# Decayed linear attention and a Mish layer: the first group's start in another order

## The chip, the cores and the metric

The kernel runs on one core of one Trainium2 chip. The metric is the device time of one execution in microseconds (us); lower is better. The kernel before takes 210.04 us, the median of 3 runs (209.95 to 210.83).

## The reference

Four sequences of 768 tokens and 8 heads of 64 go through linear attention with one decay per head, in blocks, and then through a layer with the activation h * tanh(softplus(h)), which is Mish. Cut to what matters:

```python
Dmask = np.where(rel >= 0, lam[:, None, None] ** rel[None], 0.0)
for b in range(nb):                              # blocks of a sequence
    intra = (einsum('bhic,bhjc->bhij', qb, kb) * Dmask) @ vb
    inter = einsum('bhid,bhde->bhie', qb * lam_pow, kv_state)
    out[:, :, block_b] = intra + inter
    kv_state = lam_block * kv_state + einsum('bhsd,bhse->bhde', kb * rev_pow, vb)
x = out, tokens by 512
h = x @ w_in                                     # 512 x 2048
return (h * tanh(softplus(h))) @ w_out           # 2048 x 512
```

## The kernel before, in words

The kernel takes blocks of 128 tokens, so a sequence has six, and the six make six **groups** of 4 x 128 tokens, one block from each of the four sequences. A block of one sequence is called a chunk here; chunks 0 to 3 are the first group. A chunk holds q, k and v of 8 heads, 128 tokens by 512 values. For each group the attention output is laid out transposed in `xt`; sixteen products with w_in (`mm1_unit`, into the bank `ph`, ended by Mish on ScalarE) and then products with w_out follow. The attention of the next group is laid between the products of this one. Only the first group has nothing to hide behind: its attention is the start of the kernel, and the change is about it.

The program order on every engine is written out by hand (a manual schedule), so each engine takes its instructions in the order of the code, and waits on semaphores for what others give.

The first group's decay is not taken from a running state, since the state is zero. Its mask is made whole instead: `decays` (line 182) makes rel * ln(lam) on VectorE, one piece for each of 8 heads, and ScalarE makes the exponential of four heads at a time (687, 690). The result is `dm`, in two halves t = 0 and 1. Then each chunk goes through three helpers:

- `first_t` (211) transposes k into the PSUM tile `pk` and q into `pq`, four products with the identity each; ScalarE copies pk to `pkT`, VectorE copies pq to `pqT`.
- `first_s` (228) makes the scores `pS`, eight products, and VectorE multiplies them with `dm` into `sb`, two instructions.
- `first_o` (241) makes `pO` from sb and v (`vz`), eight products, and ScalarE copies it to `xt`. pk, pq and pO have one bank each.

`busy(m)` (161) issues m products of zeros that nobody reads, 512 columns wide; they stand where TensorE would wait. Lines 684 to 713 set these in order. `mm1_part` (line 488 on) does a part of the products with w_in: for the first two tiles the 384 columns of chunks 0 to 2 are done ahead of the last `first_o`, or right behind it.

`pair_decays` (188) prepares the decay by pairs of heads, `lnp` on VectorE and its exponential `lbc` on ScalarE; `lk` (694) is the decay of k by position, from the iota `ek`. They are wanted only later, by `scale_k` and by the state's factor `lbm` (715 to 718).

All loads that turn 32-bit values into 16-bit ones go out from POOL (GpSimd) in the order of lines 125 to 146; one issue follows another on that engine. The chunks' k, q and v come first (line 69, 77, 80; 128 KB each), then w_in in four quarters `win` (the first of them in three pieces, of 128, 128 and 256 columns, line 93), then w_out in four quarters `wout`, then the second group. An issue takes its turn among eight semaphores, so that the ninth waits for the first to land. The first k and q come through SyncE and ScalarE (66, 74).

Of the kernel before, what the change touches and what calls it, by code (L numbers as in the profile page):

```python
# [20 lines left out]
def kernel(  # L21
# [62 lines left out]
    cuts = (0, 128, 256, DF // WS)  # L84
    win0 = [const.tile([128, NKC, b_ - a_], F16, name=f"win0{a_}") for a_, b_ in zip(cuts, cuts[1:])]
    win = [None] + [const.tile([128, NKC, DF // WS], F16, name=f"win{s}") for s in range(1, WS)]
    wout = [const.tile([128, NKI // WS, DMO], F16, name=f"wout{s}") for s in range(WS)]

    def load_win(s):
        w = DF // WS  # L90
        if s == 0:
            for t, a_, b_ in zip(win0, cuts, cuts[1:]):
                nc.gpsimd.dma_start(
                    out=t, in_=moe_w_in[:, a_:b_].rearrange("(k p) f -> p k f", p=128))
            return
        nc.gpsimd.dma_start(
            out=win[s],
            in_=moe_w_in[:, s * w : (s + 1) * w].rearrange("(k p) f -> p k f", p=128),
        )
# [31 lines left out]
    for f, i in ((load_q, 1), (load_v, 0), (load_k, 2), (load_q, 2)):  # L131
        f(i)
    nc.gpsimd.iota(ek, pattern=[[0, 1]], base=MID, channel_multiplier=-1,
                   allow_small_or_imprecise_dtypes=True)
# [26 lines left out]
    def busy(m):  # L161

        t = ps.tile([128, 4 * C], F32, name="busy", tag="ph", bufs=2)
        for _ in range(m):
            nc.tensor.matmul(t, kzero, kzero2, start=True, stop=True)  # L165
# [13 lines left out]
    lbc = const.tile([128, JP], F32, name="lbc")  # L179
    lqt = const.tile([128, H], F32, name="lqt")  # L180

    def decays(t):
        for j in range(JP):
# [4 lines left out]
    def pair_decays():  # L188
        lnh = lnb.rearrange("p (j t) -> p j t", t=2)
        for hp in range(2):  # L190
            rs = slice(64 * hp, 64 * hp + 64)
            nc.vector.tensor_copy(lnp[rs, :], lnh[rs, :, hp])
        nc.scalar.activation(lbc, lnp, AF.Exp, scale=float(C))
# [17 lines left out]
    def first_t(c):  # L211

        out_ = []
        for src, name in ((k0 if c == 0 else kn[c], "pk"), (q0 if c == 0 else qn[c], "pq")):
# [7 lines left out]
            if name == "pk":  # L222
                nc.scalar.activation(out_[-1], pt, AF.Copy)
# [264 lines left out]
    def mm1_part(n, ni, lo, hi):  # L488
# [4 lines left out]
        for kc in range(NKC):  # L493
            nc.tensor.matmul(  # L494
                ph_t[ni][:, lo:hi],
                win0[min(ni, 2)][:, kc, max(ni - 2, 0) * 128 : max(ni - 2, 0) * 128 + 128] if ni < w
                else win[ni // w][:, kc, (ni % w) * 128 : (ni % w) * 128 + 128],
# [185 lines left out]
    nh = len(first_halves)  # L683
    nc.scalar.activation(k0, kn[0], AF.Copy)
    decays(0)
    nc.vector.tensor_copy(q0, qn[0])
    nc.scalar.activation(dm[:, 0], dm[:, 0], AF.Exp)
    decays(1)
# [149 lines left out]
```

## Time and profile before

| what | value |
|---|---|
| median of 3 runs | 210.04 us (209.95 to 210.83) |
| the profiled execution | 210.5 us |
| its span, first to last instruction | 208.5 us |
| TensorE busy | 197.3 us (95%) |
| VectorE busy | 136.5 us (65%) |
| ScalarE busy | 90.2 us (43%) |
| POOL busy | 108.5 us (52%) |
| granted TensorE clock, mean | 0.984 |
| chain of waits, by engine | PE 73%, DVE 12%, DMA 6%, issue 4% |

In the profile, PE is TensorE's products, PEld its weight loads, DVE is VectorE, ACT is ScalarE, SP is SyncE. Times count from the span's start. A timeline row gives start, length, engine, line, operation, the tiles (out<-in), the shape and the count, and in brackets how long the engine had stood idle and what ended it. The profiled execution is one that was not among the three timed runs; terms worked out from its rows belong to its 210.5 us. "Granted clock" is the share of full speed that TensorE was given.

### The profile page before, as it was taken

The page shows a single profiled execution, that of the slowest core. Times are in us where ns is not written, and L with a number is a line of the kernel's source. Part 1 is how long each engine was busy: PE and PEld are TensorE (multiplying, and loading weights), DVE is VectorE, ACT ScalarE, POOL GpSimd, SP SyncE. Part 2 cuts the span into 40 slices and gives each one's busy share as a digit, 9 for nine tenths or more (in the row PEclk, how much of TensorE's full clock was granted, in tenths as well). Part 3 has the DMA queues.
Part 4 walks back from the last instruction along what each step waited for, and adds up shares of the span by engine and source line. Part 5 has one row for each costly group of instructions (what it writes and reads, how often), then busy time and mean ns, then how long its engine had stood idle before and what let it go on. Part 6 is the DMA issues. An engine that isn't in the chain of part 4 may idle for free.

```text
span 208.5 us, 4364 instructions
## 1 busy us (share of the span) xinstructions
PE 197.3 (95%) x1736; PEld 128.6 (62%) x1736; DVE 136.5 (65%) x253; ACT 90.2 (43%) x159; POOL 108.5 (52%) x132
## 2 busy tenths in 40 slices
PE   7598999999998999999999999999999999999993
PEld 2366544467644568845578845578755598544892
DVE  5747761577899998546997537995728784222543
ACT  4444768566672532044542055442065520366300
POOL 7997333799999799539997049970000000000000
PEclk9759999999999999999999999999999999999999
DMA  9999999999999399997999994999462222400023
GB/s 128 137 153 176 208 206 195 153 211 131 160 183 165 25 95 137 196 204 157 100 129 148 210 174 69 98 141 199 104 176 53 50 41 75 139 0 3 2 78 124
DMA packets 112470, 26.76 MB, mean 128 GB/s; under 512 B 102594, under 2 KB 111938, under 8 KB 112450
## 3 DMA queue, kind: packets, MB, share of 16 engines
q0 software_dynamic: 78080, 13.37, 87.7%
q1 hardware_dynamic: 31392, 10.49, 26.4%
q10 hardware_dynamic: 2978, 2.62, 4.1%
q8 instruction: 13, 0.21, 0.4%
q14 instruction: 7, 0.06, 0.1%
HBM read 27.26 MB, written 6.29 MB: 161 GB/s over the span
## 4 chain that ended last, share of the span: by engine, by line
PE 73%; DVE 12%; DMA 6%; issue 4%; POOL 2%; ACT 1%; ACTq 0%; DVEq 0%
PE ph L494 28%; PE z L599 13%; PE x L599 8%; PE y L599 7%; PE po L516 6%; DMA vz<-in_v_dram 4%; DVE sb L427 3%; DVE raw L393 2%; DVE xtok L446 2%; DMA qn<-in_q_dram 2%; PE fin L599 2%; DVE gsum L572 1%; PE pO L249 1%; PE pO L438 1%; PE pS L411 1%
## 5 line engine op out<-in xcount | busy, mean ns | idle before, releaser
L494 PE MATMUL ph<-xt,win 128*128 128x512 f16 (+2 forms) x404 | 88.6, 369 | 0.4 <-ACT hsg L508 0.2
L508 ACT ACTIVATE hsg<-ph 128x512 f16<-128x512 f32 x96 | 57.0, 597 | 70.4 <-PE ph L494 70.3
L494 PEld LDWEIGHTS <-win 128*128 128x128 f16 x404 | 37.0, 98 | 37.6 <-issue 0.6
L599 PEld LDWEIGHTS <-gsum 128*128 128x128 f16 x336 | 31.6, 98 | 3.5
L395 POOL TENSOR_TENSOR w<-raw,lbm 128x256 f16<-128x256 f32 x24 | 18.6, 805 | 16.7 <-DVE raw L393 16.7
L427 DVE TENSOR_TENSOR sb<-pS,maskT 128x512 f16<-128x512 f32 x32 | 19.8, 680 | 9.8 <-PE pS L411 9.8
L572 DVE TENSOR_TENSOR gsum<-hsg 128x1024 f16<-128x1024 f16 x20 | 18.6, 932 | 10.9 <-ACT hsg L508 10.9
L599 PEld LDWEIGHTS <-hsg 128*128 128x128 f16 x240 | 23.2, 98 | 3.7
L80 POOL DMA_DIRECT2D vz<-in_v_dram x24 | 21.9, 916 | 4.5 <-DMA win<-in_moe_w_in_dram 2.5
L69 POOL DMA_DIRECT2D kn<-in_k_dram x23 | 21.0, 914 | 4.9 <-DMA win<-in_moe_w_in_dram 2.4
L77 POOL DMA_DIRECT2D qn<-in_q_dram x23 | 20.9, 908 | 4.5 <-DMA wout<-in_moe_w_out_dram 3.3
L599 PE MATMUL x<-wout,hsg 128*128 128x256 f16 x160 | 19.6, 273 | 0.0
L599 PE MATMUL z<-tsum,gsum 128*128 128x256 f16 x160 | 19.1, 272 | 0.0
L264 DVE TENSOR_TENSOR ktil<-kn,lk 128x512 f16<-128x512 f16 (+1 forms) x12 | 11.3, 960 | 6.5 <-DMA kn<-in_k_dram 6.5
L516 PE MATMUL po<-wout,hsg 128*128 128x512 f16 x64 | 15.1, 379 | 0.0
L264 POOL TENSOR_TENSOR ktil<-kn,lk 128x512 f16<-128x512 f16 x12 | 13.2, 1103 | 0.0
L446 DVE TENSOR_TENSOR xtok<-pO,lqt 128x256 f16<-128x256 f32 x32 | 11.3, 412 | 0.9 <-PE pO L438 0.9
L393 DVE TENSOR_TENSOR raw<-pv,w 128x256 f32<-128x256 f32 x24 | 8.6, 414 | 4.6 <-PE pv L385 4.4
L516 PEld LDWEIGHTS <-hsg 128*128 128x128 f16 x64 | 6.0, 98 | 5.9
L599 PE MATMUL z<-tsum,hsg 128*128 128x256 f16 x80 | 9.6, 273 | 0.0
L650 DVE TENSOR_TENSOR u<-z,p 128x512 f32<-128x512 f32 x5 | 3.5, 692 | 9.0 <-PE z L599 9.0
L165 PE MATMUL busy<-kzero 128*128 128x512 f16 x18 | 7.9, 534 | 1.2 <-DVE kzero L150 1.2
(101 smaller groups left out, 220.1 us busy)
## 6 DMA issues: line engine op xcount, KB each, us to landing
out_dram<-osum SPq DMA_DIRECT2D x14, 256.0 KB, 2.5
vz<-in_v_dram POOLq DMA_DIRECT2D x24, 128.0 KB, 5.5
kn<-in_k_dram POOLq DMA_DIRECT2D x23, 128.0 KB, 5.4
qn<-in_q_dram POOLq DMA_DIRECT2D x23, 128.0 KB, 5.5
wout<-in_moe_w_out_dram POOLq DMA_DIRECT2D x4, 512.0 KB, 17.2
win<-in_moe_w_in_dram POOLq DMA_DIRECT2D x3, 512.0 KB, 10.9
out_dram<-osum ACTq DMA_DIRECT2D x5, 256.0 KB, 4.5
out_dram<-osb ACTq DMA_DIRECT2D x4, 256.0 KB, 5.9
```

Of the source, the lines that this page charges most:

```text
L69: nc.gpsimd.dma_start(out=kn[i], in_=chunk_rows(k, i))
L77: nc.gpsimd.dma_start(out=qn[i], in_=chunk_rows(q, i))
L80: nc.gpsimd.dma_start(out=vz[i % NVB][:, :, 0:D], in_=chunk_rows(v, i))
L264: (nc.vector if i <= B or 2 * B < i < 3 * B or i >= (NG - 1) * B else nc.gpsimd).tensor_tensor(out=t, in0=kn[i], in1=bc(lk, 2, D), op=ALU. ...
L395: nc.gpsimd.tensor_tensor(out=wst[b][hf][(n + 1) % 2], in0=raw, in1=lbm[:, hs, :], op=ALU.mult)
L427: nc.vector.tensor_tensor(out=s.sb[m][t], in0=sc[m][t], in1=bc(maskT, 1, JP), op=ALU.mult)
L446: nc.vector.tensor_tensor(out=xtok[m][:, :, t, :], in0=s.pO[t][:, m], in1=bc(lt[:, :, t], 2, D), op=ALU.mult)
L494: nc.tensor.matmul(ph_t[ni][:, lo:hi], win0[min(ni, 2)][:, kc, max(ni - 2, 0) * 128 : max(ni - 2, 0) * 128 + 128] if ni < w else win[ni // ...
L508: nc.scalar.activation(hsg[n][:, ni, :], ph_t.pop(ni), AF.Mish)
L516: nc.tensor.matmul(po, hsg[n][:, ki, b * C : (b + 1) * C], wout[part][:, kk, :], start=(ki == 0), stop=(ki == NKI - 1),)
L572: nc.vector.tensor_tensor(out=gsum[n, i][:, ks, :], in0=a, in1=b, op=op)
L599: nc.tensor.matmul(t, lhs(kk, b), rhs(kk, c, c + w), start=(fresh and kk == 0 and (alone or i == 0)), stop=(kk == HK - 1), skip_group_chec ...
```

## The change

Four things are changed, all in the start.

1. **Loads.** w_in's first quarter is one tile and one load, and it is issued ahead of the load of v of chunk 3; the iota ek comes right behind the iota rel.
2. **Decay.** The exponential of 128 * ln(lam) is made for all heads (`lbh`) right behind the logarithm, and so is `lk`; `pair_decays` only copies on VectorE, and stands behind the last products of the first group. Seven of the eight pieces of `decays` come before q's conversion, one behind it. The table for Mish is loaded right behind dm's second exponential.
3. **Order.** The transposes of chunk 1 come right behind the scores of chunk 0, and those of chunk 3 come before the pO of chunk 1.
4. **Zero products.** `busy` can be given a width. Of the products of 512 columns many are gone; products of 128 columns stand in the pauses: two before the first transposes, four between those of k and of q, four before the scores of chunk 2, two before the pO of chunk 2.

```diff
-    cuts = (0, 128, 256, DF // WS)
-    win0 = [const.tile([128, NKC, b_ - a_], F16, name=f"win0{a_}") for a_, b_ in zip(cuts, cuts[1:])]
-    win = [None] + [const.tile([128, NKC, DF // WS], F16, name=f"win{s}") for s in range(1, WS)]
+    win = [const.tile([128, NKC, DF // WS], F16, name=f"win{s}") for s in range(WS)]
...
-    for f, i in ((load_q, 1), (load_v, 0), (load_k, 2), (load_q, 2)):
-        f(i)
     nc.gpsimd.iota(ek, pattern=[[0, 1]], base=MID, channel_multiplier=-1,
                    allow_small_or_imprecise_dtypes=True)
-    for f, i in ((load_v, 1), (load_k, 3), (load_q, 3), (load_v, 2), (load_v, 3)):
+    for f, i in ((load_q, 1), (load_v, 0), (load_k, 2), (load_q, 2), (load_v, 1), (load_k, 3),
+                 (load_q, 3), (load_v, 2), (load_win, 0), (load_v, 3)):
         f(i)
-    for s in range(WS):
+    for s in range(1, WS):
         load_win(s)
...
-    def busy(m):
+    def busy(m, w=4 * C):
...
-            nc.tensor.matmul(t, kzero, kzero2, start=True, stop=True)
+            nc.tensor.matmul(t[:, 0:w], kzero, kzero2[:, 0:w], start=True, stop=True)
...
     def pair_decays():
-        lnh = lnb.rearrange("p (j t) -> p j t", t=2)
-        for hp in range(2):
-            rs = slice(64 * hp, 64 * hp + 64)
-            nc.vector.tensor_copy(lnp[rs, :], lnh[rs, :, hp])
-        nc.scalar.activation(lbc, lnp, AF.Exp, scale=float(C))
+        for src, dst in ((lnb, lnp), (lbh, lbc)):
+            lnh = src.rearrange("p (j t) -> p j t", t=2)
+            for hp in range(2):
+                rs = slice(64 * hp, 64 * hp + 64)
+                nc.vector.tensor_copy(dst[rs, :], lnh[rs, :, hp])
...
             if name == "pk":
+                if between:
+                    busy(between, C)
                 nc.scalar.activation(out_[-1], pt, AF.Copy)
...
+    nc.scalar.activation(lbh, lnb, AF.Exp, scale=float(C))
+    nc.scalar.activation(lk, lnb, AF.Exp, scale=ek)
     nc.scalar.activation(k0, kn[0], AF.Copy)
-    decays(0)
+    decays(0, range(JP))
+    decays(1, range(JP - 1))
     nc.vector.tensor_copy(q0, qn[0])
+    decays(1, range(JP - 1, JP))
     nc.scalar.activation(dm[:, 0], dm[:, 0], AF.Exp)
-    decays(1)
-    first_t(0)
+    busy(2, C)
+    first_t(0, between=4)
     nc.scalar.activation(dm[:, 1], dm[:, 1], AF.Exp)
+    nc.scalar.preload_act_table(AF.Mish)
     busy(1)
     first_s(0)
-    pair_decays()
-    nc.scalar.activation(lk, lnb, AF.Exp, scale=ek)
+    first_t(1)
     busy(2)
-    first_t(1)
-    nc.scalar.preload_act_table(AF.Mish)
-    busy(1)
     first_s(1)
     first_o(0)
-    busy(3)
     first_t(2)
-    busy(1)
+    busy(4, C)
     first_s(2)
+    first_t(3)
     first_o(1)
-    busy(3)
-    first_t(3)
+    busy(2, C)
     first_o(2)
-    busy(1)
     first_s(3)
     mm1_part(0, 0, 0, GT - C)
     first_o(3)
     mm1_part(0, 1, 0, GT - C)
     scale_k(0)
+    pair_decays()
```

Three places in the engines' rows show what stands where. First ScalarE, from the logarithm (lnb) to the transposed k of chunk 1, before:

```order
L173 ACTIVATE lnb<-lamb 128x8
L684 ACTIVATE k_94<-kn_98 128x512
L687 ACTIVATE dm<-dm 128x512
L223 ACTIVATE pkT<-pk 128x512
L690 ACTIVATE dm<-dm 128x512
L193 ACTIVATE lbc<-lnp 128x4
L694 ACTIVATE lk<-lnb,ek 128x8
L223 ACTIVATE pkT<-pk 128x512
L697 ACT_TABLE_LOAD
L251 ACTIVATE xt<-pO 128x4x128
```

The same place in the changed kernel:

```order
L165 ACTIVATE lnb<-lamb 128x8
L678 ACTIVATE lbh<-lnb 128x8
L679 ACTIVATE lk<-lnb,ek 128x8
L680 ACTIVATE k_92<-kn_96 128x512
L685 ACTIVATE dm<-dm 128x512
L218 ACTIVATE pkT<-pk 128x512
L688 ACTIVATE dm<-dm 128x512
L689 ACT_TABLE_LOAD
L218 ACTIVATE pkT<-pk 128x512
L246 ACTIVATE xt<-pO 128x4x128
```

The two small exponentials have gone from between dm and the second pkT to the place behind the logarithm, and the table load now stands ahead of the second pkT.

Second POOL, from the load of v of chunk 1 (vz_70) to w_out, before:

```order
L133 IOTA ek 128x1
L80 DMA vz_70<-in_v_dram 128x8x64
L69 DMA kn<-in_k_dram 128x8x64
L77 DMA qn<-in_q_dram 128x8x64
L80 DMA vz_71<-in_v_dram 128x8x64
L80 DMA vz_72<-in_v_dram 128x8x64
L93 DMA win_77<-in_moe_w_in_dram 128x4x128
L93 DMA win_78<-in_moe_w_in_dram 128x4x128
L93 DMA win_79<-in_moe_w_in_dram 128x4x256
L96 DMA win_80<-in_moe_w_in_dram 128x4x512
```

And in the changed kernel:

```order
L80 DMA vz_70<-in_v_dram 128x8x64
L69 DMA kn<-in_k_dram 128x8x64
L77 DMA qn<-in_q_dram 128x8x64
L80 DMA vz_71<-in_v_dram 128x8x64
L89 DMA win_77<-in_moe_w_in_dram 128x4x512
L80 DMA vz_72<-in_v_dram 128x8x64
L89 DMA win_78<-in_moe_w_in_dram 128x4x512
```

Three issues have become one, and it stands ahead of v of chunk 3 (vz_72).

Third TensorE, where the transposes of chunk 3 end (qn_117 before, qn_115 in the changed kernel, are q of chunk 3). Before:

```order
L217 MATMUL pq_352<-ident_89,qn_117 128x128
L217 LDWEIGHTS qn_117
L217 MATMUL pq_352<-ident_89,qn_117 128x128
L249 LDWEIGHTS vz2_71
L249 MATMUL pO_359<-sb_327,vz2_71 128x128
```

In the changed kernel:

```order
L210 MATMUL pq_338<-ident_87,qn_115 128x128
L210 LDWEIGHTS qn_115
L210 MATMUL pq_338<-ident_87,qn_115 128x128
L244 LDWEIGHTS vz1_70
L244 MATMUL pO_345<-sb_283,vz1_70 128x128
```

Behind these transposes stood the pO of chunk 2 (vz2); now the pO of chunk 1 (vz1) stands there.

More of the change, by code (lines that the diff above doesn't have):

```diff
@@ L179, with decays @@
     lbc = const.tile([128, JP], F32, name="lbc")
+    lbh = const.tile([128, H], F32, name="lbh")
     lqt = const.tile([128, H], F32, name="lqt")
-    def decays(t):
-        for j in range(JP):
+    def decays(t, js):
+        for j in js:
             nc.vector.scalar_tensor_tensor(
@@ L209, with first_t @@
     sb0 = {}
-    def first_t(c):
+    def first_t(c, between=0):
         out_ = []
```

8 lines of the change are left out of this document (1 added, 7 removed).

## The prediction

> **What bounds the kernel now.** I read the page's slices first, then the chain of waits, because the change touches only the first 20 us and the loads behind them.
>
> ```profile
> PEclk9759999999999999999999999999999999999999
> ```
>
> One slice is 5.2 us. TensorE runs at full clock everywhere except in slices 2 and 3, where the change works. The chain of waits, in order of time, shows what the start hangs on:
>
> ```profile
> 5.81 1.05 DVE dm L184 x4
> ...
> 7.24 0.43 PE pS L235 x8
> ...
> 9.41 0.29 ACT lk L694
> ...
> 10.24 0.61 PE pS L235 x6
> ...
> 11.81 1.28 PE busy L165 x3
> ...
> 14.46 0.56 PE pS L235 x8
> ...
> 19.04 0.55 PE pO L249 x7
> 19.59 0.65 PE ph L494 x4
> ```
>
> It is a ping-pong: transposes, copy, score product pS, masking sb, output product pO, four times over. Once it is over (19.04) dense products follow. Four entries are work that the change moves or drops: dm behind q (1.05 us), the small exponential lk, the zero products (1.28 us), and the place of pS. The clock, by stretches of 3.41 us (columns: stretch, length, busy time of PE, weight loads, DVE, ACT, POOL; then granted clock, DMA share, GB/s):
>
> ```profile
> 4.60:8.01 3.41, 1.77 (x19) 1.03 (x20) 2.09 (x7) 1.92 (x4) 3.41 (x5) 1.00 2.32 148
> 8.01:11.43 3.42, 2.68 (x25) 1.89 (x24) 2.22 (x6) 2.11 (x4) 3.42 (x5) 0.50 2.10 134
> 11.43:14.84 3.41, 3.32 (x24) 1.97 (x22) 1.17 (x3) 1.25 (x3) 3.41 (x6) 0.50 2.02 151
> 14.84:18.25 3.41, 3.27 (x44) 2.30 (x40) 2.27 (x4) 1.79 (x3) 3.41 (x6) 1.00 1.20 155
> ```
>
> The clock changes exactly at these borders. Behind a stretch with 1.77 us busy (52%) it fell to half; behind 2.68 (78%) it stayed there; behind 3.32 (97%) it came back. So it takes between 78% and 97% to come back; it falls at 52% and holds at 96% (3.27, the last row), and between these two nothing is known.
>
> **The change, part by part.** *Up to the first pS.* The rows, of DVE and ACT:
>
> ```profile
> 3.42 1.14 DVE L184 SCALAR_TENSOR_TENSOR dm<-rel,lnb,gone 128x128 f32<-128x128 f32 x4 [0.42 <-ACT lnb L173]
> ...
> 4.18 0.63 ACT L684 ACTIVATE k<-kn 128x512 f16<-128x512 f32 x1 [0.79 <-DMA kn<-in_k_dram]
> ...
> 5.38 0.43 DVE L686 CAST q<-qn 128x512 f16<-128x512 f32 x1 [0.82 <-DMA qn<-in_q_dram]
> ...
> 6.78 0.42 DVE L225 COPY pqT<-pq 128x512 f16<-128x512 f16 x1
> ...
> 7.73 1.29 DVE L239 TENSOR_TENSOR sb<-pS,dm 128x512 f16<-128x512 f32 x2 [0.54 <-PE pS L235]
> ...
> 8.94 0.33 DVE L192 COPY lnp<-lnb 64x4 f32<-64x4 f32 x2
> ...
> 9.30 0.21 ACT L193 ACTIVATE lbc<-lnp 128x4 f32<-128x4 f32 x1 [1.78 <-DVE lnp L192]
> ...
> 9.61 0.58 ACT L223 ACTIVATE pkT<-pk 128x512 f16<-128x512 f16 x1
> 10.20 1.28 ACT L697 ACT_TABLE_LOAD   x1
> ...
> 11.85 0.60 ACT L251 ACTIVATE xt<-pO 128x512 f16<-128x512 f32 x1 [0.37 <-PE pO L249]
> ```
>
> A dm piece is 1.14/4 = 0.285 us. Seven of them now run in DVE's wait for q: 3.42 + 7 x 0.285 = 5.42, against the 5.38 at which q starts today, a loss of 0.04. Then q (0.43) to 5.85, its transposes to about 6.3, and pqT at 6.35 instead of 6.78, since one dm piece stands ahead of it and not four. The first pS starts at 6.8 and not at 7.24: **0.4 sooner**. The two small exponentials now ahead of k0 (0.21 and 0.29, rows of lbc and lk) end near 3.9, and k0 waits for its load until 4.18: they cost nothing.
>
> *Up to the second pS.* Today ACT stands 1.78 us before lbc, which waits for lnp behind sb on DVE; pkT of chunk 1 queues behind it. Both are gone. Instead the table load (1.28) comes forward: dm's second exponential ends near 6.8, the load at 8.1, pkT at 8.7. DVE is now the later one: sb from 7.3 to 8.6, pqT to 9.0. The second pS starts at 9.05 and not at 10.24: **1.2 sooner**. If the table load were slower, pkT would take over from pqT: a cushion of 0.35.
>
> *Up to the third pS and on.* The rows of TensorE, the first three at half clock:
>
> ```profile
> 10.78 1.04 PE L249 MATMUL pO<-sb,vz 128*128 128x128 f16 x8
> 11.61 1.49 PE L165 MATMUL busy<-kzero 128*128 128x512 f16 x3
> ...
> 13.31 0.63 PE L217 MATMUL pq<-ident,qn 128*128 128x128 f16 x4
> ...
> 19.43 0.81 PE L494 MATMUL ph<-xt,win 128*128 128x384 f16 x4
> ```
>
> A product group's tail overlaps with the next (11.61 - 10.78 = 0.83 of pO's 1.04). At half clock: pS at 9.05, pO at 9.6 to 10.65, xt (0.60) to 11.27, pkT behind it to 11.9, so pS of chunk 2 at 11.9 and not 14.46: 2.5 sooner, also because three zero products (1.28) no longer stand there. Then TensorE meets loads.
>
> ```profile
> L77 POOL DMA_DIRECT2D qn<-in_q_dram x1: 893/893/893, 8.1 to 8.1; - x1
> DMA to landing us min/median/max: 4.5/4.5/4.5
> ```
>
> This is q of chunk 3 (the first row is the issue, in ns; the second its way to landing): 8.14 + 4.5 = 12.6. Its issue comes some 0.15 sooner, since the ek iota no longer stands ahead of it; call it 12.45. The transposes of chunk 3 now stand **ahead** of pO of chunk 1, so that pO waits for this load: it starts at 12.9 and ends at 14.0, its xt at 14.6, and as pO has one bank, pO of chunk 2 starts at 14.65, pS of chunk 3 at 15.5, sb of chunk 3 ends at 17.4. The last xt that ph needs is there at 16.3: ph (0.65 at full clock by the chain, 1.3 at half) runs from 16.35 to 17.6, the last pO from 17.6. Of the 2.5 us, 1.4 are left (19.04 against 17.6).
>
> *The weights.* Of POOL and its loads:
>
> ```profile
> 6.29 0.16 POOL L133 IOTA ek<- 128x1 f32 x1
> ...
> 10.74 2.28 POOL L93 DMA_DIRECT2D win<-in_moe_w_in_dram  x3
> ...
> L80 POOL DMA_DIRECT2D vz<-in_v_dram x2: 903/908/913, 9.0 to 9.9; - x2
> DMA to landing us min/median/max: 4.4/4.7/4.9
> ...
> L93 POOL DMA_DIRECT2D win<-in_moe_w_in_dram x3: 795/799/803, 10.7 to 12.2; - x3
> DMA to landing us min/median/max: 4.7/4.7/6.4
> ...
> L96 POOL DMA_DIRECT2D win<-in_moe_w_in_dram x3: 812/820/828, 12.9 to 14.4; - x3
> DMA to landing us min/median/max: 8.2/10.9/12.7
> ```
>
> v of chunk 2 lands at 9.0 + 4.4 = 13.4, v of chunk 3 at 14.8, the quarter's last piece at 12.2 + 6.4 = 18.6, the second quarter at 12.9 + 8.2 = 21.1: a whole quarter takes 21.1 - 18.6 = 2.5 us of the stream. Two issues (2 x 0.76) are saved and the whole quarter starts behind v of chunk 2, itself 0.1 sooner: it lands near 13.3 + 2.5 = 15.8, v of chunk 3 near 16.7 (a 128 KB load follows another by 0.85), the second quarter near 19.3, **1.9 sooner**. So the first ph waits for 512 KB in place of 128 (15.8 and not 15.4), and the last pO for a v that is 1.9 later than now: at half clock both are there before 16.35 and 17.6; at full clock they set the start. The far bound, if the stream gains no more than the two issues, is 18.6 - 1.5 = 17.1, and costs 0.7 of the 1.4; I take 15.8, since the next quarter's 2.5 us is the nearest row.
>
> *The clock decides the rest.* In the second stretch (4.60 to 8.01) I count pk with its small products 0.6, pq with busy 0.65, pS, transposes and two products 1.15: 2.4 us or 70%, between the 52% that fell and the 96% that held: open. If it falls, the next stretch holds 2.5 to 2.9 us (pS, pO, transposes and small products from 9.0 on), no more than about the 78% that did not bring it back; the one up to 14.84 holds some 2.5 (pS 0.6, transposes 0.6 beyond the wait, pO 1.0, small ones 0.3). If it holds, the next stretch has only 1.9 (55%), so it falls at 11.43. Either way I expect **half clock until 18.25**, where it is full today from 14.84: the small products are too small, a quarter of those they replace. The ph and pO products above are taken at half clock for that reason; the last pO has 0.65 of its 0.83 behind it at 18.25, the rest runs at full clock, and the next ph starts at 18.4, against 19.43: **1.05 sooner**, and all is dense behind it.
>
> [...]
>
> *Later.* What is behind must not take it back:
>
> ```profile
> 38.51 0.69 DVE L264 TENSOR_TENSOR ktil<-kn,lk 128x512 f16<-128x512 f16 x1 [6.50 <-DMA kn<-in_k_dram]
> 62.78 0.38 PE L385 MATMUL pv<-vz,ktil 128*128 128x128 f16 x4 [0.42 <-DMA vz<-in_v_dram]
> 56.00:64.00 8.00, 7.25 (x54) 4.05 (x52) 8.00 (x7) 4.73 (x9) 7.95 (x9) 1.00 1.84 186
> ```
>
> ktil waits for a load that stands behind all weights, so it comes sooner by what the weights gain (1.9); TensorE comes 1.05 sooner, so nothing new waits there. The wait of 0.42 at 62.78 shrinks as loads gain 0.85 more than TensorE, but DVE is busy 8.00 of 8.00 us there, so I count 0.1 of it. The four tiny copies that now stand ahead of lbm (two of lnp take 0.33, so four 0.66) lie on DVE while TensorE runs ph: nothing; without that cover they would cost 0.66.
>
> Sum: 0.4, then 1.2, then 2.5, shrunk to 1.4 by the q load and to 1.05 by the clock, plus 0.1: **1.15 us**. The profiled execution took 210.5 us (span 208.5), 0.46 above the median of 210.04; the sum against it is 209.35, against the median **208.9**.
>
> **The rivals.**
>
> *Full clock at the end of the start.* The clock is back at 14.84 or never falls. For it: 70% is far above 52%. Against it: the small products. Then pS of chunk 3 comes at 15.1, sb ends at 16.9, the last pO is held by it and by v (16.7), the next ph starts at 17.4, 2.0 sooner; the loads, 1.9 sooner, cap it. Time 210.04 - 1.9 = 208.1.
>
> *Half clock for one stretch more: slower.* If the quarter lands at the lower bound (17.1) or later, ph starts there, the last pO at 18.4, the stretch up to 18.25 is idle for over a fifth, the clock stays at half up to 21.66, and dense products lose 3.41/2 = 1.7 us against my forecast; the later start takes 0.4 more. Time 208.9 + 2.1 = 211.0. It decides from a landing of about 17. Against it: the stream's rows above.
>
> *It does not do what it says.* TensorE gets ahead, but DVE and POOL, both full from 56 to 64, give it back, as their shift against each other can lengthen DVE's work there: 210.0, give or take 0.4.
>
> **How the numbers follow.** Forecast (half clock to 18.25) 50%, 208.4 to 209.4; full clock 23%, 207.7 to 208.5; given back 14%, 209.6 to 210.4; slower 13%, 210.4 to 211.5. The range 207.9 to 210.6 leaves out about a fifth: the lower part of the second and most of the last. A difference of 0.5% (1.05 us, the least that a measurement can tell) divides at 208.99 and 211.09. Faster by more: 0.55 of the first case and nearly all of the second, 0.50. Slower by more: half of the last case and some for what I overlook, 0.12. Within: 0.38.
>
> **What would show it.** pS starts at 6.8, 9.05, 11.9 and 15.5; pq of chunk 3 waits for the load of q, pO behind it; the clock's rows at half from 8.01 or 11.43 to 18.25; the first quarter landing near 15.8, the second near 19.3; ktil's load near 36.6. I would be wrong if the clock is full by 15 us (then 208.1), if ph waits for w_in past 17, or if the lead of about 1.05 at the second ph is gone at 64 us.

## The result: no change

The changed kernel takes 210.14 us, the median of 20 runs (208.51 to 211.46), the kernel before 209.91 us in its 20 runs beside it (208.91 to 211.59). The ratio is 1.000, its 95% interval 0.9978 to 1.0022. I had forecast 208.9: the time lies within the range that I gave (207.9 to 210.6), but the gain of 1.15 us isn't there. The profiled execution of the changed kernel took 210.33 us, its span 208.6. Here and below the medians are of all executions, while the intervals leave out those more than 1.5% above a kernel's fastest: none of these 20, but up to six of 12 in the experiments (i1), so that where the two disagree the median is the safer of them.

The start did what the change is meant to do, up to the last third of it. TensorE's timeline in the changed kernel:

```profile
6.99 0.40 PE L230 MATMUL pS<-pqT,pkT 64*128 64x128 f16 x8
...
9.15 0.40 PE L230 MATMUL pS<-pqT,pkT 64*128 64x128 f16 x8 [0.77 <-DVE pqT L220]
...
11.28 0.40 PE L230 MATMUL pS<-pqT,pkT 64*128 64x128 f16 x8 [0.51 <-ACT pkT L218]
...
12.52 0.40 PE L210 MATMUL pq<-ident,qn 128*128 128x128 f16 x4 [0.46 <-DMA qn<-in_q_dram]
...
14.60 0.40 PE L230 MATMUL pS<-pqT,pkT 64*128 64x128 f16 x8
17.41 1.46 PE L489 MATMUL ph<-xt,win 128*128 128x384 f16 x4 [2.41 <-DMA win<-in_moe_w_in_dram]
18.66 1.06 PE L244 MATMUL pO<-sb,vz 128*128 128x128 f16 x8
19.52 2.58 PE L489 MATMUL ph<-xt,win 128*128 128x384 f16 x16
```

The four pS start at 6.99, 9.15, 11.28 and 14.60, where the kernel before had them at 7.24, 10.24, 14.46 and 17.26: a lead of 2.66 us at the fourth. Then TensorE stands for 2.41 us until w_in's first quarter is there, and the lead is gone: the second row of ph (19.52) is 0.09 later than before (19.43). The chain of waits says the same; of its rows from 9 to 22 us:

```profile
...
9.74 7.62 DMA win<-in_moe_w_in_dram
17.36 0.05 issue
17.41 1.46 PE ph L489 x4
18.87 0.85 PE pO L244 x8
```

What held the start before was a ping-pong of engines. What holds it now is one load, issued at 9.74 and landed at 17.36. Of that load's group, the issues and the way to landing (the first of the three is this quarter):

```profile
L89 POOL DMA_DIRECT2D win<-in_moe_w_in_dram x3: 807/827/828, 9.7 to 12.1; - x3
...
DMA to landing us min/median/max: 7.6/9.4/11.2
```

And the stretches of the clock (columns as in the prediction):

```profile
6.79:10.20 3.41, 2.55 (x40) 1.92 (x40) 2.40 (x6) 1.90 (x3) 3.41 (x5) 1.00 2.19 140
10.20:13.61 3.41, 2.31 (x37) 1.63 (x34) 2.66 (x6) 1.83 (x4) 3.41 (x6) 1.00 1.92 155
13.61:17.03 3.42, 0.95 (x16) 0.67 (x16) 1.98 (x5) 0.98 (x2) 2.27 (x4) 1.00 1.51 191
17.03:20.44 3.41, 3.03 (x15) 1.89 (x16) 2.24 (x7) 0.60 (x1) 1.94 (x4) 0.50 1.26 203
20.44:23.85 3.41, 3.41 (x26) 1.94 (x25) 1.05 (x3) 2.28 (x4) 1.14 (x2) 1.00 1.25 207
```

The clock was full through the pS, with 75% and 68% of a stretch busy. It fell after the stretch in which TensorE waited for w_in (0.95 of 3.42 us, 28%), so that dense products then ran at half. In the page's slices it shows in one digit:

```profile
PEclk9996999999999999999999999999999999999999
```

A half stretch, wherever it lies, can be counted in the timed runs too, since each lists its mean clock: one stretch of 3.41 us at half takes 3.41 / 2 / 208.6 = 0.8% off it. A mean under 0.9955 had 17 of the changed kernel's 20 executions and 38 of 157 of the kernel before (in five sets of runs). What the half stretch costs can't be read from this: the three executions of the changed kernel above 0.9955 lie at 208.51, 209.40 and 211.46, and the six whose mean (0.982 to 0.984) speaks of two half stretches have a median of 210.38, only 0.24 above the 11 at 0.989 to 0.992 (210.14), where a whole stretch of dense products at half would cost 3.41 / 2 = 1.7 us.

### The profile page after: what moved, and what is told of

It is laid out like the page before. It is cut to its first block, busy times and chain, and to the rows that moved or that the text cites. A ratio compares the mean times of both kernels' runs of the same rounds, so it can differ in the third digit from the quotient of the medians.

```text
span 208.6 us, 4368 instructions
## 1 busy us (share of the span) xinstructions
PE 195.5 (94%) x1739; PEld 128.1 (61%) x1739; DVE 135.7 (65%) x255; ACT 90.2 (43%) x159; POOL 107.3 (51%) x130
## 4 chain that ended last, share of the span: by engine, by line
PE 76%; DVE 8%; DMA 6%; POOL 4%; issue 2%; ACT 2%; ACTq 0%; POOLq 0%; DVEq 0%; SPq 0%
PE ph L489 32%; PE z L593 13%; PE x L593 8%; PE y L593 7%; PE po L510 7%; DMA win<-in_moe_w_in_dram 4%; DMA kraw<-ktil 3%; DVE sb L422 2%; DVE raw L388 2%; PE fin L593 2%; DVE xtok L441 1%; POOL kn L69 1%; POOL qn L77 1%; PE pS L406 1%; POOL vz L80 1%
## 5 line engine op out<-in xcount | busy, mean ns | idle before, releaser
L489 PE MATMUL ph<-xt,win 128*128 128x512 f16 (+2 forms) x404 | 89.6, 372 | 2.6 <-DMA win<-in_moe_w_in_dram 2.4
L390 POOL TENSOR_TENSOR w<-raw,lbm 128x256 f16<-128x256 f32 x24 | 18.6, 804 | 17.2 <-DVE raw L388 17.1
L566 DVE TENSOR_TENSOR gsum<-hsg 128x1024 f16<-128x1024 f16 x20 | 19.2, 958 | 10.9 <-ACT hsg L502 10.9
L259 DVE TENSOR_TENSOR ktil<-kn,lk 128x512 f16<-128x512 f16 (+1 forms) x12 | 10.5, 895 | 4.6 <-DMA kn<-in_k_dram 4.6
L566 DVE TENSOR_TENSOR gsum<-hsg,gsum 128x1024 f16<-128x1024 f16 x10 | 7.6, 801 | 2.1 <-PE z L593 2.1
```

What stands on the lines that cost most here:

```text
L259: (nc.vector if i <= B or 2 * B < i < 3 * B or i >= (NG - 1) * B else nc.gpsimd).tensor_tensor(out=t, in0=kn[i], in1=bc(lk, 2, D), op=ALU. ...
L390: nc.gpsimd.tensor_tensor(out=wst[b][hf][(n + 1) % 2], in0=raw, in1=lbm[:, hs, :], op=ALU.mult)
L489: nc.tensor.matmul(ph_t[ni][:, lo:hi], win[ni // w][:, kc, (ni % w) * 128 : (ni % w) * 128 + 128], xt[n][:, kc, lo:hi], start=(kc == 0), s ...
L566: nc.vector.tensor_tensor(out=gsum[n, i][:, ks, :], in0=a, in1=b, op=op)
```

## The experiments

Three theories. **L**: the start's lead is spent on the load queue, where the first ph or the last pO waits for what lands late. **C**: the small zero products let the clock fall. **D**: VectorE and POOL give a lead back after 50 us. Lead below is the start of the same ScalarE instruction on `hsg` (tile 5 of the first group, tile 7 and tile 13 of the second, the last tile) in the profile of before (23.73, 62.17, 71.28, 192.72) minus its start in this profile. It compares single executions: the profile of before had two half stretches in its start, and g1, which has the same start, leads it by 1.32 us at 24 us. So a lead of that size is not yet a gain of the new order.

| kernel | median us (runs) | ratio to before, 95% | lead at 24, 62, 71, 193 us |
|---|---|---|---|
| changed | 210.14 (20) | 0.9978 to 1.0022 | -0.36, -0.36, +0.41, -0.28 |
| e1 pieces | 210.24 (12) | 0.9978 to 1.0040 | -0.99, -1.00, +0.06, -0.32 |
| e2 old loads | 208.83 (12) | 0.9895 to 0.9961 | +1.38, +1.37, -1.02, -0.22 |
| e3 loads alone | 209.53 (12) | 0.9936 to 0.9985 | -0.30, -0.31, +1.10, +0.53 |
| e4 filled wait | 210.42 (12) | 0.9989 to 1.0060 | -0.98, -0.98, +1.05, -0.30 |
| f1 halves | 209.31 (12) | 0.9929 to 0.9996 | +1.30, +1.11, +1.02, +1.03 |
| f2 no zeros | 211.08 (12) | 0.9953 to 1.0044 | +1.26, +1.25, -1.74, -1.36 |
| f3 v sooner | 209.59 (12) | 0.9945 to 1.0001 | +1.81, +1.49, +0.23, +0.15 |
| f4 v sooner, before | 209.71 (12) | 0.9961 to 1.0021 | -0.52, -0.53, +0.48, +0.47 |
| g1 sums later, before | 209.65 (12) | 0.9932 to 0.9994 | +1.32, +1.32, +2.90, +1.79 |
| g2 sums later, old loads | 208.52 (12) | 0.9902 to 0.9973 | +1.84, +1.83, +3.19, +2.07 |
| g3 sums later, changed | 210.27 (12) | 0.9956 to 1.0029 | -1.84, -1.85, +0.18, -0.96 |
| g4 sums later, halves | 208.83 (12) | 0.9911 to 0.9975 | +2.23, +2.20, +3.38, +1.76 |
| h1 whole, behind v | 211.22 (12) | 0.9987 to 1.0052 | -3.13, -3.15, -1.12, -1.11 |
| h2 one piece | 210.66 (12) | 0.9943 to 1.0024 | +1.89, +1.88, +2.55, +2.49 |
| i1 old loads again | 210.81 (12) | 0.9916 to 1.0004 | +1.73, +1.73, +0.52, -0.19 |
| i2 one piece again | 210.44 (12) | 0.9972 to 1.0041 | +1.17, +1.16, -0.05, -0.05 |
| i3 sums later, one piece | 209.10 (12) | 0.9914 to 0.9971 | +1.24, +1.24, -2.81, -3.63 |

### The load: its size and its place

**e1**, the quarter in pieces at its new place:

```diff
...
+        if s == 0:
+            for t, a_, b_ in zip(win0, cuts, cuts[1:]):
+                nc.gpsimd.dma_start(
+                    out=t, in_=moe_w_in[:, a_:b_].rearrange("(k p) f -> p k f", p=128))
+            return
...
```

> The changed kernel with w_in's first quarter in its three pieces again, at the new place ahead of v of chunk 3. Theory L (the lead of the start is spent waiting for a whole quarter of w_in, which lands late): the first ph waits for the first piece alone and starts near 15.5 and not 17.4; but v of chunk 3, behind three pieces, lands near 18, so the last pO waits there: 0.3 to 0.8 us faster than before. Theory C (the lead is spent by half clock, since the zero products are too small): the first ph starts sooner, but the clock falls all the same: within 0.3 us of before. Theory D (DVE and POOL give it back after 50 us): a lead of 0.5 us or more at 22 us that is gone at 70 us.

Measured: 210.24 us, nothing gained. TensorE's timeline in this kernel:

```profile
13.41 0.40 PE L217 MATMUL pq<-ident,qn 128*128 128x128 f16 x4 [1.37 <-DMA qn<-in_q_dram]
...
16.23 1.44 PE L496 MATMUL ph<-xt,win 128*128 128x384 f16 x4
18.22 1.03 PE L251 MATMUL pO<-sb,vz 128*128 128x128 f16 x8 [0.55 <-DMA vz<-in_v_dram]
```

The first ph no longer waits, but v of chunk 3 now lies behind all three pieces, and the last pO starts at 18.22. The clock was half from 15.43 to 22.25, behind a stretch (12.01 to 15.43) that was 43% busy. In it TensorE waited 1.37 us for q of chunk 3, which landed at 13.36 here and at 12.47 in the changed kernel; so this fall came ahead of the first ph. Pieces at this place gained nothing.

**e2**, the changed kernel with the loads as before (e1's pieces, behind v of chunk 3; the iota ek stays early):

```diff
...
-                 (load_q, 3), (load_v, 2), (load_win, 0), (load_v, 3)):
+                 (load_q, 3), (load_v, 2), (load_v, 3)):
...
-    for s in range(1, WS):
+    for s in range(WS):
...
```

> The changed kernel with the loads as before: three pieces, behind v of chunk 3 (ek stays early). Theory L: first ph near 15.5, last pO near 16.5 to 17, a lead of 1.5 to 2 us at the second ph, cut by the last piece and the second quarter (near 18.5 and 21): 1.0 to 1.7 us faster than before. Theory C: no more than 0.3 us faster. Theory D: the lead is there at 22 us and gone at 70 us, time within 0.3 us of before.

Measured: 208.83 us, faster than before. ph starts at 15.58, the last pO at 16.24, and the lead at 24 us is 1.38. This speaks for L. But its own profiled execution (210.36) had lost the lead by 71 us, and the same kernel, run again as i1 below, comes out at 210.81.

**e3**, the kernel before with the load part alone (the quarter as one tile and one load, and this order):

```diff
...
-    for f, i in ((load_q, 1), (load_v, 0), (load_k, 2), (load_q, 2)):
-        f(i)
...
-    for f, i in ((load_v, 1), (load_k, 3), (load_q, 3), (load_v, 2), (load_v, 3)):
+    for f, i in ((load_q, 1), (load_v, 0), (load_k, 2), (load_q, 2), (load_v, 1), (load_k, 3),
+                 (load_q, 3), (load_v, 2), (load_win, 0), (load_v, 3)):
...
```

> The kernel before with the load part alone: the whole quarter ahead of v of chunk 3, ek early. Theory L: the first ph is ready at 17.8 and the quarter lands near 17.4, v of chunk 3 near 18.3, the last pO is ready near 19: at most 0.3 us slower or faster. If the landing were as early as forecast (15.8), the same. Theory D would have the later part gain from weights that land 0.4 to 1.5 us sooner: 0 to 0.5 us faster. Theory C: no change.

Measured: 209.53 us, 0.4% faster. With the old, later start nothing waits for the quarter (landed at 16.37, ph at 18.11). The second quarter lands at 19.76 and not 21.16. So the load part, which costs the changed start its lead, does no harm where the start is late, and by the interval gains a little. The lead also rises, from -0.31 at 62 us to +1.10 at 71, but that can't be put down to these loads: all seven profiles that are behind at 62 us gain 0.8 to 2.0 us up to 71, f4 with the old loads of w_in among them (-0.53 to +0.48). So it seems to be the profile of before, from which the lead is counted, that loses time there.

**f1**, the quarter in two halves, v of chunk 3 between them:

```diff
...
-                 (load_q, 3), (load_v, 2), (load_win, 0), (load_v, 3)):
+                 (load_q, 3), (load_v, 2), (load_half, 0), (load_v, 3), (load_half, 1)):
...
```

> The changed kernel with w_in's first quarter as two loads of 256 columns, v of chunk 3 issued between them. Theory L (the start's lead is spent on the load queue: everything issued behind or beside the whole quarter lands late, and the pause this makes is also what lets the clock fall): the first half lands near 16 us, so the first ph no longer stands 2.4 us, but v of chunk 3 and the second half still land at 17 to 18, so part of the pause comes back at the last pO: between the two, 209.3 to 209.9. Theory C (the small zero products are what lets the clock fall, wherever loads land): no change, 210.1. Theory D (DVE and POOL give any lead back after 50 us): no change, 210.1, whatever the lead is at 22 us.

Measured: 209.31 us, at the edge of what L had; ph starts at 16.02, the last pO at 16.91.

**h1**, the whole quarter again, but behind v of chunk 3:

```diff
-                 (load_q, 3), (load_v, 2), (load_win, 0), (load_v, 3)):
+                 (load_q, 3), (load_v, 2), (load_v, 3), (load_win, 0)):
```

> The changed kernel with the load of w_in's whole first quarter behind v of chunk 3, as it stood before, and not ahead of it. In pieces ahead of v of chunk 3 the quarter gave 210.24 us, in pieces behind it 208.83. Theory P (the place alone costs: v of chunk 3 lands behind 512 KB, at 18.2 us, and holds the last pO): v lands near 14.9, so 208.7 to 209.2. Theory S (the size costs as well: the first ph needs 128 columns but waits for 512): the quarter lands near 17.4, ph starts there, the pause before it is over 2 us and the clock falls behind it in most executions, 209.6 to 210.2.

Measured: 211.22 us, and a mean clock under 0.9955 in all 12 executions. The chain and TensorE's timeline of this kernel:

```profile
10.54 9.37 DMA win<-in_moe_w_in_dram
```

```profile
19.95 1.46 PE L489 MATMUL ph<-xt,win 128*128 128x384 f16 x4 [5.12 <-DMA win<-in_moe_w_in_dram]
```

The load takes 9.37 us to land, 5.12 of them with TensorE idle: worse than both theories had. So the size costs by itself, and P, the place as the only cause, falls. The second quarter, issued 0.74 us behind it, landed 1.85 us behind it (21.76 against 19.91), where quarters that follow one another land 2.5 apart. My reading of these landings, an estimate, is that loads in flight share the stream, so that one isn't done before the next have taken part of it. The load ahead shows the same: v of chunk 2 lands at 13.17 to 13.66 where a load of 128 KB is issued right behind it (before and 11 others), and at 13.82 to 14.68 where one of 256 or 512 KB is (changed, e3, e4, f1, g3, g4); e1, where q was late, has 14.20 with 128 KB behind it. How the stream is shared no run shows.

**h2**, one piece of 128 columns ahead of v of chunk 3, two behind:

```diff
...
-                 (load_q, 3), (load_v, 2), (load_win, 0), (load_v, 3)):
+                 (load_q, 3), (load_v, 2), (load_piece, 0), (load_v, 3),
+                 (load_piece, 1), (load_piece, 2)):
...
```

> The changed kernel with the quarter in pieces, the first piece (128 columns) ahead of v of chunk 3 and the other two behind it. What lies ahead of v is 128 KB and not 512. Theory P: the first piece lands near 14.9 and v near 15.7, neither is waited for longer than with the old loads (0.6 us before the first ph there): 208.3 to 208.9. Theory S: the same. If any w_in load ahead of v of chunk 3 harms: 209.5 or more.

TensorE's timeline in the profiled execution, which took 207.77 us:

```profile
15.55 0.81 PE L497 MATMUL ph<-xt,win 128*128 128x384 f16 x4 [0.36 <-ACT xt L254]
...
16.57 0.55 PE L252 MATMUL pO<-sb,vz 128*128 128x128 f16 x7 [0.15 <-DVE sb L242]
16.95 2.64 PE L497 MATMUL ph<-xt,win 128*128 128x384 f16 x16
```

No load holds the start, and the second row of ph is 2.5 us sooner than before (19.43). Yet the median is 210.66 us: the executions lie near 208 (three) or above 209.6 (nine). This profile is the fastest of the 12, so it shows that the start can be free of waits, and not what the nine lost; i2 below, the same kernel, shows an execution of 210.32 that led at 24 us all the same.

### The zero products and the clock

**f2**, e2 without zero products in the pauses:

```diff
...
-    busy(2, C)
-    first_t(0, between=4)
+    first_t(0)
...
-    busy(1)
...
-    busy(2)
...
-    busy(4, C)
...
-    busy(2, C)
...
```

> The changed kernel with the loads as before (208.83 us in the earlier run) and with all zero products of the pauses taken out, only the first six kept. Theory C: the pauses are then bare, the clock falls in the start and dense products lose up to 1.7 us for each stretch of 3.41 at half: 210 to 211. Theory L: the real products and transposes alone carry a stretch to 60 per cent or so, and no stretch is as empty as the one that waited for the whole quarter (28 per cent): 208.6 to 209.2, clock full or one stretch at half where hardly anything runs.

Measured: 211.08 us, the time that C had. TensorE's timeline in this kernel:

```profile
12.36 0.61 PE L237 MATMUL pS<-pqT,pkT 64*128 64x128 f16 x8 [0.52 <-DVE pqT L227]
...
13.73 1.06 PE L251 MATMUL pO<-sb,vz 128*128 128x128 f16 x8
...
16.01 0.40 PE L237 MATMUL pS<-pqT,pkT 64*128 64x128 f16 x8
```

The third pS takes 0.61 us, as the one at 10.24 of before, in a stretch at 0.50, and the fourth 0.40. In eleven other profiles of the changed order (changed, e1, e2, e4, f1, f3, g2, g3, g4, h1, h2) the third, at 11.02 to 11.45, already takes 0.40. So in this execution the start without zero products ran at half clock for longer. But that isn't where the time went: its lead at 24 us is 1.26, about that of e2 with zero products (1.38), and it was lost between 62 and 71 us, where TensorE waited 1.18 and 2.07 us for v of the third group. The median is 0.3 from that of i1, the same kernel with zero products (210.81, on another chip). That the zero products are needed for the time is not shown. Nor are the small ones of the change always enough for the clock: in e1 and e4 it fell in the start ahead of the first ph (at 15.43 and 14.70).

**e4**, ten wide zero products in the wait for w_in:

```diff
     first_s(3)
+    busy(10)
     mm1_part(0, 0, 0, GT - C)
```

> The changed kernel with ten zero products of 512 columns in the wait ahead of the first ph (2.2 us at full clock, some 0.3 of it may lie beyond the wait). Theory C: the clock no longer falls at the end of the start, dense products lose nothing to half clock: 1.0 to 1.5 us faster than the changed kernel. Theory L: the wait for the quarter stays, the first ph still starts near 17.4 and only the half clock behind it goes: 0.5 to 1.2 us faster than the changed kernel in those executions in which the clock fell, nothing in the others. Theory D: no change.

Measured: 210.42 us. Only 2 of 12 executions had a mean clock under 0.9955, so the filling does hold the clock. It gains nothing: the ten others have a median of 210.19, against 210.14 of the changed kernel, 17 of whose 20 lost the clock. The profiled execution is one of the two. Here the clock had fallen at 14.70, ahead of the filling, behind a stretch (11.28 to 14.70) that was 51% busy and held a wait of 1.03 us for v of chunk 2:

```profile
16.24 3.23 PE L157 MATMUL busy<-kzero 128*128 128x512 f16 x10
19.31 0.81 PE L489 MATMUL ph<-xt,win 128*128 128x384 f16 x4
```

Begun at half clock, which lasts until 18.11, the ten products take 3.23 us, and ph, whose weights landed at 17.23, starts 2.1 us behind them. Whether the filling holds ph in the ten executions at full clock, no profile shows; there it would end earlier, as three such products take 0.81 us at full clock and 1.49 at half (before, at 15.41 and 11.61).

### From 62 to 71 us

**f3** and **f4**: v of the third group's first two chunks loaded ahead of k and q of its last two, in e2 and in the kernel before:

```diff
-    ahead += [(lambda i=i: load_v(i)) for i in third]
+    ahead[4:4] = [(lambda i=i: load_v(i)) for i in third[:2]]
+    ahead += [(lambda i=i: load_v(i)) for i in third[2:]]
```

> The changed kernel with the loads as before, and in the third group the loads of v of its first two chunks issued behind the k and q of these chunks and not behind all four k and q. The profile showed TensorE waiting there at 62 us for v (0.42 us in the kernel before). Theory L (loads set the place at 62 too): 0.3 to 0.5 us less than with the loads as before alone, 208.4. Theory D (DVE and POOL, both full there, set it): no change, 208.8, or worse, since k of chunk 10 comes 1.7 us later: up to 209.3.

> The kernel before with only that order of the third group's loads. Theory L: 0.3 to 0.4 us less than before, 209.5. Theory D: no change, 209.9, or up to 210.3.

Measured: 209.59 and 209.71 us. In f3 VectorE now waits 2.38 and 2.66 us for k, at 57.60 and 61.07; what v gains, k loses. Neither shows a gain.

**g1 to g4**: four sums of w_out's quarters (`tsum`, VectorE, 128 x 1024) stood at 58 to 67 us; they go to 80 us, in the kernel before, in e2, in the changed kernel and in f1:

```diff
-            if n == 1 and 4 <= u < 8:
-                weight_sum(1 if u < 6 else 3, u % 2)
+            if n == 1 and 18 <= u < 22:
+                weight_sum(1 if u < 20 else 3, u % 2)
```

> The kernel before with four sums of w_out's quarters (tsum, VectorE, second group) 14 tiles later, at about 80 us, where VectorE has idle time; at 61 to 67 us, where they stood, VectorE and POOL are both full and TensorE waits for VectorE. Theory D (VectorE beside POOL sets the time at 62 to 70 us, so that whatever lead the start has ends there): some 0.5 to 1.5 us faster, 208.5 to 209.4. Theory T (it is the third group's loads and transposes through the DMA queues that set it, the v and k of these chunks): no change, 209.9.

> The changed kernel with the loads as before and the four sums later. Its start led by 1.4 to 1.8 us at 62 us in the profiles and kept none of it or little at 70. Theory D: the lead gets through: 1.2 to 1.8 us less than the kernel before with the sums later, 206.9 to 207.9. Theory T: 208.8 to 209.4, no better than without moving the sums.

> The changed kernel with the four sums later. Theory D together with L (its start has no lead, since it waits 2.4 us for the whole quarter; and VectorE beside POOL sets 62 to 70 us): like the kernel before with the sums later, 208.5 to 209.4, and 1.2 us or more above the changed kernel with the old loads and the sums later. Theory T: no change, 210.1.

> The changed kernel with w_in's first quarter in two halves, v of chunk 3 between them, and the four sums later. Theory D: its lead of 1.1 us at 62 us gets through, 207.3 to 208.3. Theory T: its loads land 1 us sooner than with the old loads, so it keeps more than that one does: 209.0 to 209.4, as without moving the sums.

Measured: 209.65, 208.52, 210.27 and 208.83 us. All four ran on one chip. D's gain in the kernel before is small (0.1 to 0.7% by the interval). But the lead now gets through: in the profiles of g2 and g4 it is 1.8 and 2.2 us at 62 and 2.1 and 1.8 at the end. The changed kernel with its whole quarter (g3) has none to bring through, and stays at 210.27. This is the cleanest test of L: g2 and g4 differ from g3 in the loads of w_in's first quarter alone, and 10 and 11 of their 12 executions are under 209.8, of g3's only 3.

**i1, i2, i3**: e2, h2, and h2 with the sums later, on one chip; the edits are those above.

> The changed kernel with the loads as before, once more, beside the next two on the same chip. If the load order alone makes the difference between it (208.83 us) and the one with a single piece ahead of v of chunk 3 (210.66, measured on another chip): 208.5 to 209.2 here. If the time of both is one mixture of executions that keep the start's lead through 62 to 70 us and of others that lose it: the two come out within 0.8 us of each other here, both between 208.5 and 210.7.

> The changed kernel with one piece of w_in ahead of v of chunk 3 and two behind it, once more. Its profile had no wait for w_in or v at the start and led by 1.9 us at 24 us and 2.5 at the end, at 207.77 us, while its median was 210.66. Load order: 210.2 to 211. Mixture: within 0.8 us of the one with the old loads.

> The same with the four sums 14 tiles later, at about 80 us. If VectorE's sums beside POOL's work at 62 to 68 us are where executions lose the lead (theory D): a half to two us below the same kernel without that, few executions above 210. If not: the same median, within 0.4 us.

Measured: 210.81, 210.44 and 209.10 us. The old loads and the one piece come out alike, as the mixture had it. e2 and i1 are one kernel on one chip, and their medians, 208.83 and 210.81, differ by 2.0 us: where executions lie near 208 or above 209.6, as in h2, 12 of them can fall mostly to one side. So a median of one such set (208.83 of e2, 209.31 of f1) shows little by itself. Where an execution loses the lead, the rows show. VectorE in i1, then POOL, then TensorE:

```profile
62.28 1.40 DVE L395 TENSOR_TENSOR raw<-pv,w 128x256 f32<-128x256 f32 x4
63.60 2.89 DVE L555 TENSOR_TENSOR tsum<-wout,tsum 128x1024 f16<-128x1024 f16 x1
66.42 2.47 DVE L429 TENSOR_TENSOR sb<-pS,maskT 128x512 f16<-128x512 f32 x4
```

```profile
63.84 3.23 POOL L397 TENSOR_TENSOR w<-raw,lbm 128x256 f16<-128x256 f32 x4
```

```profile
67.15 0.38 PE L387 MATMUL pv<-vz,ktil 128*128 128x128 f16 x4 [1.82 <-DVE sb L429]
```

In h2, which kept its lead, the same sum and the same four products of POOL:

```profile
63.19 1.12 DVE L556 TENSOR_TENSOR tsum<-wout,tsum 128x1024 f16<-128x1024 f16 x1
```

```profile
64.12 2.84 POOL L398 TENSOR_TENSOR w<-raw,lbm 128x256 f16<-128x256 f32 x4
```

One instruction takes 2.89 us in place of 1.12, sb behind it is as much later, and TensorE waits 1.82 us. e2 (2.89, wait 1.82) and i2 (2.89, wait 1.82) have rows alike; in all three the sum begins 0.24 to 0.25 us ahead of POOL's four products, in h2 0.93 ahead and nearly done. In the kernel before it begins 0.82 us behind POOL's first product, and takes 1.13 (VectorE, then POOL):

```profile
65.88 1.13 DVE L553 TENSOR_TENSOR tsum<-wout,tsum 128x1024 f16<-128x1024 f16 x1
65.06 3.23 POOL L395 TENSOR_TENSOR w<-raw,lbm 128x256 f16<-128x256 f32 x4
```

That is longer too, only less: the four sums at 39 to 41 us of before, where POOL issues loads and no products, take 0.68 to 0.69. Another sum of 128 x 1024, `gsum`, does alike in before: 0.68 us at 103.48 and 106.48, where POOL issues loads, and 2.96 at 99.27, where it begins 0.28 us ahead of four products of POOL (VectorE, then POOL):

```profile
99.27 2.96 DVE L572 TENSOR_TENSOR gsum<-hsg 128x1024 f16<-128x1024 f16 x1
...
103.48 0.68 DVE L572 TENSOR_TENSOR gsum<-hsg 128x1024 f16<-128x1024 f16 x1
...
106.48 0.68 DVE L572 TENSOR_TENSOR gsum<-hsg 128x1024 f16<-128x1024 f16 x1
```

```profile
99.55 3.26 POOL L395 TENSOR_TENSOR w<-raw,lbm 128x256 f16<-128x256 f32 x4
102.76 0.94 POOL L80 DMA_DIRECT2D vz<-in_v_dram  x1
103.69 0.88 POOL L69 DMA_DIRECT2D kn<-in_k_dram  x1
```

So in before the sums beside POOL's products took longer than those beside its load issues (the 1.12 of h2 lay mostly beside one); by what mechanism no run shows. How long a sum takes by where it falls is not explained here. Nor does every long sum cost the lead: f1 and h2 have one of 2.4 us at 59.31 and 58.40 and keep theirs.

Taking the sums away helps the median of this kernel (209.10 against 210.44, on the same chip), but is no full cure. i3's profiled execution took 213.74 us, its slowest by 2.9, and lost its time at the same place to something else:

```profile
61.91 0.38 PE L388 MATMUL pv<-vz,ktil 128*128 128x128 f16 x4 [1.01 <-DMA vz<-in_v_dram]
64.43 0.59 PE L388 MATMUL pv<-vz,ktil 128*128 128x128 f16 x4 [2.14 <-DMA vz<-in_v_dram]
```

```profile
60.00:63.41 3.41, 1.28 (x9) 0.50 (x6) 0.76 (x2) 1.19 (x2) 3.39 (x6) 1.00 1.83 153
63.41:66.82 3.41, 2.39 (x9) 1.15 (x10) 0.75 (x2) 0.06 (x1) 2.52 (x4) 0.50 1.69 160
66.82:70.24 3.42, 3.42 (x38) 1.81 (x37) 0.81 (x2) 1.14 (x2) 1.09 (x2) 0.50 1.49 92
```

v of the third group came late, TensorE was busy 1.28 of 3.41 us, and the clock fell for two stretches. f2's profile has the same two waits, of 1.18 and 2.07 us, and half clock from 65.85 to 69.27. So two things can take the lead here, a sum beside POOL and a late v with the clock behind it. What makes v late in one execution and not in another stays open.

Put together: the six kernels with a leading start and the sums in place (e2, f1, f3, h2, i1, i2) have 72 executions, of which 22 are under 209.2 us and 24 at 210.4 or above; their median is 209.93, against 210.01 of 157 executions of the kernel before. The changed kernel has 210.14. So with the sums in place, taking the wait for w_in away shows no clear gain. The three with the sums later (g2, g4, i3) have 36, 24 of them under 209.2, with a median of 208.88, 0.5% under before. The best of all, g2 at 208.52 (0.9902 to 0.9973), lies below both kernels, but it is picked as the best of 17 from 12 executions, and its interval overlaps with that of g1 (209.65), which has the start of before. That the new order of the start is worth anything beside the later sums is not shown.

## Why the prediction was wrong

- **pS.** Right in the order and in the first two. Forecast 6.8, 9.05, 11.9, 15.5; measured 6.99, 9.15, 11.28, 14.60. The last two were 0.6 and 0.9 sooner: I had taken their terms at half clock, and it was full. pq of chunk 3 did wait for q (12.52, forecast 12.45).
- **The weights: the step that failed.** I took 15.8 for the landing of w_in's first quarter, from 2.5 us for "a whole quarter of the stream" behind v of chunk 2, and wrote that at half clock the quarter and v "are there before 16.35 and 17.6". The quarter landed at 17.36 and v at 18.27. v of chunk 2 came at 14.01, not 13.3, and the quarter took 3.35 us more. In the three other profiles with this load order (e3, e4, g3) v came at 13.82 to 14.68 and the quarter 2.55 to 2.92 behind it, at 16.37 to 17.44. So the first term of my sum was too small in every profile, the second in two of the four. The bound that I put aside as the far one (17.1) was the nearer one. The 2.5 us is the distance of two large loads that overlap; it isn't how long one takes to land: from issue it took 7.6 us here and 9.4 in h1. My own rows could have told: the last piece (256 columns, 256 KB) landed at 18.6, the piece ahead of it at 11.5 + 4.7 = 16.2, so half a quarter took 2.4 us as well. The second quarter came at 20.76, not 19.3.
- **The clock.** Wrong in mechanism. I expected half clock until 18.25 because the small products are too small. It was full until 17.03, through stretches that were 75% and 68% busy, and fell behind the wait for w_in. Nearest to it is the rival "half clock for one stretch more", which I had decided from a landing of 17 and given 13%: its landing came true, but the clock fell at 17.03 and was back at 20.44, where the rival had it stay down from before up to 21.66. It priced 211.0, and the time came out at 210.14. The start ahead of the wait was 0.9 us sooner at the fourth pS than I had it; what the half stretch itself cost the executions don't show.
- **The base.** My terms came from an execution with half clock from 8.01 to 14.84. In g1, with the same start as before, the clock was full from 9.69, and its lead at 24 us is 1.32:

```profile
10.73 0.40 PE L235 MATMUL pS<-pqT,pkT 64*128 64x128 f16 x8 [0.84 <-ACT pkT L223]
...
18.10 2.32 PE L494 MATMUL ph<-xt,win 128*128 128x384 f16 x16
```

  In the four profiles of the start of before (before, e3, f4, g1) its second row of ph lies between 18.10 and 19.95. So a part of the gain that I forecast at the start was the clock of one execution.
- **Given back by DVE and POOL.** In the changed kernel there was no lead to give back. Where there was one (e2, i1, i2), this rival happened as told, a little later than I put it (at 64 to 67 us, not 56 to 64), by one instruction of 2.89 us. Without the wait for w_in my 208.9 would still have been the time of only some executions: 22 of the 72 above are under 209.2.

## What to carry to other kernels

A load merged from pieces, or moved ahead in a queue, is to be priced by when its last byte lands with everything that is issued next in the stream beside it (the whole quarter took 7.62 us in the changed kernel, 9.37 in h1); ask what the first reader needs, and load that by itself (in h2 this took the wait away). A wait can have half clock behind it, as those of 2.41 us in the changed kernel, 1.37 in e1 and 1.03 in e4 had; what that adds to the time is to be measured, as here it didn't show in the executions. And read a start from more than one execution, since the clock's stretches began elsewhere each time (a border at 4.60 in before, at 6.79 in the changed kernel), and repeat a set of runs before a difference of a few tenths is believed.

## What the runs showed of the hardware

- The stretches of the clock are 3.41 us long in the profiles of before, the changed kernel, e4 and i3, and lie differently in each: a border is at 4.60 in before, 6.79 in the changed kernel, 11.28 in e4 and 60.00 in i3, no two of them a whole number of stretches apart.
- At full clock the changed kernel kept the clock behind stretches that were 75% and 68% busy, and lost it behind one of 28%; it was lost behind 37% in i3, 43% in e1, 51% in e4 and 52% in before. These are single stretches, and no rule is read from them.
- A granted clock of 1.00 at the start of a profile need not be a reading: f2's view has 1.00 for 11.70 to 15.10, beside a pS of 0.61 us (12.36), which in before (10.24) goes with 0.50.
- The same kernel on the same chip spreads by 3 us and more from run to run (i1: 207.81 to 213.18), and the medians of two sets of 12 by 2.0 (e2 and i1).
